# Sparse attention with a SoLU feed-forward layer: the first strided values loaded as two column halves for 128 partitions, not as two partition halves

## The chip, the cores and the metric

The kernel runs on one core of one Trainium2 chip. The metric is the device time of one execution in microseconds (us); lower is better. A core has five engines that run side by side and wait for each other by semaphores: TensorE (PE, matrix products), VectorE (DVE), ScalarE (ACT), GpSimd (POOL) and SyncE (SP). SyncE and ScalarE each issue transfers to a queue of their own; the packets of both queues are carried by the core's 16 DMA engines. SBUF is the memory on the chip, with 128 partitions; PSUM takes the products.

## The reference

Eight batches of eight heads with 576 positions and 64 elements a head. Heads 0 to 3 see the 32 latest positions ("local"), heads 4 to 7 see every 32nd earlier position ("strided"). The result goes through a feed-forward layer whose activation is x times softmax(x), with a layer norm behind it.

```python
scores = np.matmul(q, k.transpose(0, 1, 3, 2)) / np.sqrt(D)
mask_local = (rel >= 0) & (rel < 32)
mask_strided = (rel >= 0) & (pos[None, :] % 32 == pos[:, None] % 32)
scores = np.where(masks, scores, -1e9)          # heads 0-3 local, 4-7 strided
attn = softmax(scores)
x = np.matmul(attn, v)                          # -> 4608 tokens x 512
h = x @ w_in                                    # 512 -> 1024
solu = h * softmax(h)
ln = (solu - mean(solu)) / np.sqrt(var(solu) + 1e-6) * g_ln
out = ln @ w_out                                # 1024 -> 512
```

## The kernel before

The work goes by batch. A batch has five *units* of attention, two strided and then three local. A unit makes scores on TensorE (`qk`, a mask product at L512 and the scores at L517), takes the softmax on VectorE, ScalarE and GpSimd (L523 to L542), turns the probabilities by a transposing transfer (L546) and multiplies them by the values (`pv`, L568). Tiles of 128 tokens then go through the feed-forward layer (`ff`, L626 to L628 and L670 to L672, the bulk of TensorE's work).

The values are used as a high and a low fp16 part, with one scale for each batch, a power of two that is made from the squares of all values. For batch 0 the squares are summed on TensorE: `gram` (L379) multiplies each 128 columns of the raw values by themselves, 24 matmuls for the strided values and 10 for the local ones, in that order on TensorE ahead of and between the first scores.

The tile `vtwo` holds 12 x 4 x 64 float32 columns in 128 partitions. For batch 0 it holds the strided values twice: partitions 0 to 63 and 64 to 127 have the same content, and the columns are two halves y = 0, 1 of 1536. In HBM `vstr[0]` has 128 rows of 1536, row y x 64 + p. The split at L463 and L464 makes the high part for all 128 partitions, and the low part for the first 64, once for each y, without a transfer from one partition half to the other. For later batches the tile is used in another way: its first half takes the raw values (one load for 128 partitions), its second half the fp16 parts.

The order of work is written out by a planner (`Plan`): each step has an engine, a cost and a key, and the planner simulates queues to choose the order on each engine. `load` (L319) issues a transfer, on ScalarE's queue for the names in `ACTQ = {"t0", "t1"}`, which are the two loads of this case, otherwise on SyncE's queue. Steps carry names for what they read and write: `("vr", 1)` and `("vr2", 1)` are the first and the second of the two loads, and `gram` and the split are placed behind both. The semaphores themselves are set from the bytes that an instruction touches. There are eight semaphores for transfers (DMAHW0 to 7), dealt out in turn in the order of issue; the ninth transfer waits until the one that last had its semaphore is done.

At the start ScalarE issues the two loads, and SyncE issues strided `q`, the masks, strided `k`, the first `w_in` block, the local values (`vrl`), the second `w_in` block; then, with waits, `g`, local `k`, the third `w_in` block, local `q`, the fourth `w_in` block. The `w_in` blocks land in `room` and `eu` and are decoded on ScalarE and VectorE (L695 to L697).

Of the kernel before, what the change touches and what calls it, by code (L numbers as in the profile page):

```python
# [17 lines left out]
B, H, S, D = 8, 8, 576, 64  # L18
# [106 lines left out]
class Plan:  # L125
# [13 lines left out]
    def add(self, eng, dur, fn, key, r=(), w=(), lock=None, dma=None, after=()):  # L139

        n = len(self.steps)
        deps = set(after)
        for x in r:
            if x in self.writer:
                deps.add(self.writer[x])
        for x in w:
            if x in self.writer:
                deps.add(self.writer[x])
            deps.update(self.readers.get(x, ()))
        for x in r:  # L150
            self.readers.setdefault(x, []).append(n)
        for x in w:
            self.writer[x], self.readers[x] = n, []
        deps.discard(n)
        lock = eng == "pool" if lock is None else lock
        self.spaces.append({x[0] for x in (*r, *w) if isinstance(x, tuple) and x[0] in BANKED} if eng in ("pe", "act", "dve") else set())
        self.steps.append((eng, dur, fn, key, deps, lock, dma))
        return n
# [86 lines left out]
def attn_solu_kernel(ctx: ExitStack, tc: tile.TileContext, qloc, qstr, kloc, kstr, vloc, vstr, w_in, w_out, g, masks, out):  # L245
# [71 lines left out]
    def load(name, dst, src, us, key, w, after=()):  # L317
        e, q = ("act", nc.scalar) if name in ACTQ else ("sp", nc.sync)
        add(e, us, lambda: q.dma_start(dst, src), key, w=w, dma=LOAD, after=after)  # L319
# [104 lines left out]

    def load_v(b, a, key, key2=None):
        if b == 0 and a:
            for i in range(2):
                load(f"t{i}", vtwo[i * D : i * D + D].rearrange("p (y f) -> p y f", y=2), vstr[b].rearrange("(y p) f -> p y f", y=2), 1.95,
                     key2 if i else key, [("vr2", 1)] if i else [("vr", 1), ("v", 1, 0), ("v", 1, 1)])
            return  # L430
        load(f"v{a}{b}", vr_sb[a], (vloc, vstr)[a][b], (1.57, 1.93)[a], key, [("vr", a)])

# [323 lines left out]
    load_qk(0, 1, LF[0], LF[1])  # L756
    load_masks(LF[2])
    load_v(0, 1, LF[3], LF[4])
    load_v(0, 0, LF[5])
    load_qk(0, 0, LF[6], LF[7])  # L760
    load("g", g_sb, g, 0.1, LF[8], ["g"])
    prep_w()
    t = 0
    v_scale(0, VK[0])
    for b in range(B):
        if b:
            load_qk(b, 1, LK[b])
        v_split(b, 1, VK[b] + 0.5)
        for j in range(2):
            unit(b * NU + j, UK[b * NU + j], PK[b * NU + j])  # L770
        if b:
            load_qk(b, 0, LK[b] + 2)
        v_split(b, 0, VK[b] + 2.5)
        for j in range(2, NU - 1):
            unit(b * NU + j, UK[b * NU + j], PK[b * NU + j])
        if b + 1 < B:
            if b == 0:
                prep_o()
            load_v(b + 1, 1, LK[b + 1] + 0.5)
            load_v(b + 1, 0, LK[b + 1] + 2.5)  # L780
            v_scale(b + 1, VK[b + 1])
        unit(b * NU + NU - 1, UK[b * NU + NU - 1], PK[b * NU + NU - 1])
        if b == 0:
            split_o()
        while t < NT and (t * P + P - 1) // S <= b:
            ff(t, TK[t], GK[t])
            t += 1
# [63 lines left out]
```

## Time and profile before

| | |
|---|---|
| median of three runs | 514.79 us (513.05 to 514.99) |
| profiled execution | 512.79 us, span 511.1 us, mean granted clock 0.97 |
| TensorE busy | 473.5 us (93%) |
| VectorE busy | 358.5 us (70%) |
| ScalarE busy | 295.5 us (58%) |
| GpSimd busy | 157.4 us (31%) |
| moved by the DMA engines | 96.51 MB, mean 189 GB/s |

The span is one execution as the profiler records it; the profiled execution's own time contains it and what lies around it. The median of the runs stands 2.0 us above the profiled execution. A row of a group of instructions gives the line, the engine, the operation, what it writes and reads; behind it the busy time, and in brackets the idle time of its engine just before with what ended it. "SPq" and "ACTq" are the issuing sides of SyncE's and ScalarE's queues.

### The profile page before, as it was taken

The numbers are of one execution on the slowest core, as the hardware profiler recorded it, in microseconds if no ns is written. First come the engines' busy times: TensorE is split into PE (matmuls) and PEld (weight loads), VectorE is DVE, ScalarE is ACT, GpSimd is POOL, SyncE is SP. The second block draws the span as 40 slices with busy tenths as digits, with TensorE's granted clock in tenths as the row PEclk, the third lists the DMA queues.
The fourth block names the chain that finished last, engine by engine and source line by source line (L and its number), as shares of the span: only waits on it lengthen the run. The fifth ranks groups of instructions, "written<-read, shape, count | busy, mean of one in ns | idle before, by whom it ended". The sixth has DMA issues, their size and how long they took to land.

```text
span 511.1 us, 11878 instructions
## 1 busy us (share of the span) xinstructions
PE 473.5 (93%) x4858; PEld 247.2 (48%) x4858; DVE 358.5 (70%) x679; ACT 295.5 (58%) x414; POOL 157.4 (31%) x258
## 2 busy tenths in 40 slices
PE   0538978999999999999999999999999999999997
PEld 0435544445545555454544455555544555544443
DVE  0597989768767779667994789677975789754330
ACT  1578967684546737654765666564666447554331
POOL 3164363314313214313341235212531315311210
PEclk9855989999999999999999999999999999999999
DMA  8999999739993799979885499979985697673342
GB/s 218 402 310 271 355 211 202 152 77 242 273 199 84 157 211 280 222 212 195 236 161 109 118 227 239 245 202 223 231 158 104 164 167 158 108 122 63 65 104 78
DMA packets 168294, 96.51 MB, mean 189 GB/s; under 512 B 138032, under 2 KB 154800, under 8 KB 167728
## 3 DMA queue, kind: packets, MB, share of 16 engines
q1 hardware_dynamic: 162768, 84.74, 77.9%
q10 hardware_dynamic: 5472, 11.01, 6.9%
q8 instruction: 38, 0.62, 0.5%
q14 instruction: 16, 0.13, 0.1%
HBM read 40.03 MB, written 9.44 MB: 97 GB/s over the span
## 4 chain that ended last, share of the span: by engine, by line
PE 80%; DMA 7%; DVE 5%; ACT 4%; issue 2%; POOL 1%; ACTq 0%; POOLq 0%; DVEq 0%
PE h_ps L626 11%; PE o_ps L670 11%; PE h_ps L628 11%; PE h_ps L627 11%; PE o_ps L671 10%; PE o_ps L672 10%; PE s_ps L517 5%; PE x_ps L568 5%; DMA pt<-p 3%; DMA vtwo<-vstr 3%; PE s_ps L512 2%; DMA ct<-c 2%; POOL t L534 1%; ACT w L712 1%; PE s_ps L672 1%
## 5 line engine op out<-in xcount | busy, mean ns | idle before, releaser
L626 PE MATMUL h_ps<-w,xhi 128*128 128x512 f16 x280 | 107.1, 382 | 0.6 <-DVE eu L647 0.6
L627 PE MATMUL h_ps<-w,xhi 128*128 128x512 f16 x280 | 106.7, 381 | 0.0
L628 PE MATMUL h_ps<-w,xlo 128*128 128x512 f16 x280 | 106.6, 381 | 0.0
L670 PE MATMUL o_ps<-obuf,ct 128*128 128x512 f16 x272 | 103.4, 380 | 1.0 <-DMA ct<-c 1.0
L672 PE MATMUL o_ps<-obuf,ct 128*128 128x512 f16 x272 | 103.1, 379 | 0.0
L671 PE MATMUL o_ps<-obuf,ct 128*128 128x512 f16 x272 | 103.1, 379 | 0.0
L534 POOL TENSOR_TENSOR t<-t,m 128x576 f32<-128x576 f32 (+2 forms) x40 | 56.2, 1404 | 139.4 <-DVE m L531 111.4
L633 DVE TENSOR_REDUCE st<-h_ps 128x1 f32<-128x1024 f32 x35 | 42.8, 1222 | 42.5 <-PE h_ps L628 42.5
L652 DVE SCALAR_TENSOR_TENSOR c<-eu,st,c 128x1024 f16<-128x1024 f32 x36 | 48.8, 1354 | 25.3 <-ACT c L651 24.1
L644 ACT ACTIVATE eu<-h_ps,st,vsc 128x1024 f32<-128x1024 f32 x31 | 37.3, 1204 | 43.3 <-DVE st L634 43.3
L651 ACT ACTIVATE c<-eu,st 128x1024 f16<-128x1024 f32 x36 | 41.2, 1146 | 28.0 <-DVE st L650 26.0
L647 DVE SCALAR_TENSOR_TENSOR eu<-h_ps,st,eu 128x1024 f32<-128x1024 f32 x35 | 44.8, 1280 | 8.8 <-ACT eu L644 8.4
L660 POOL TENSOR_SCALAR st<-st 128x1 f32<-128x1 f32 x36 | 18.7, 520 | 103.2 <-ACT junk L654 102.0
L540 ACT CAST p<-t 128x576 f16<-128x576 f32 (+2 forms) x40 | 26.9, 674 | 33.2 <-POOL t L534 32.6
L628 PEld LDWEIGHTS <-xlo 128*128 128x128 f16 x288 | 28.3, 98 | 34.5 <-issue 0.8
L672 PEld LDWEIGHTS <-ct 128*128 128x128 f16 x288 | 28.2, 98 | 34.0
L626 PEld LDWEIGHTS <-xhi 128*128 128x128 f16 x288 | 28.2, 98 | 33.7 <-DVE eu L647 0.7
L670 PEld LDWEIGHTS <-ct 128*128 128x128 f16 x288 | 28.1, 98 | 33.1 <-DMA ct<-c 1.1
L627 PEld LDWEIGHTS <-xhi 128*128 128x128 f16 x288 | 28.3, 98 | 31.3 <-issue 0.6
L517 PE MATMUL s_ps<-k,q 64*54 64x54 f32 (+1 forms) x1280 | 41.4, 271 | 2.2 <-DMA q<-qloc 2.2
L671 PEld LDWEIGHTS <-ct 128*128 128x128 f16 x288 | 28.2, 98 | 30.2
L654 ACT ACTIVATE junk<-eu,st 128x1024 bf16<-128x1024 f32 x36 | 40.9, 1137 | 0.8 <-ACT ob L678 0.8
(148 smaller groups left out, 707.6 us busy)
## 6 DMA issues: line engine op xcount, KB each, us to landing
out<-ob ACTq DMA_DIRECT2D x36, 256.0 KB, 3.9
vtwo<-vstr SPq DMA_DIRECT2D x7, 768.0 KB, 6.6
vd<-vtwo SPq DMA_DIRECT2D x14, 384.0 KB, 8.8
vrl<-vloc SPq DMA_DIRECT2D x8, 640.0 KB, 5.6
q<-qstr SPq DMA_DIRECT2D x8, 594.0 KB, 5.4
k<-kstr SPq DMA_DIRECT2D x8, 594.0 KB, 6.8
k<-kloc SPq DMA_DIRECT2D x8, 576.0 KB, 6.0
q<-qloc SPq DMA_DIRECT2D x8, 576.0 KB, 4.2
```

Of the source, the lines that this page charges most:

```text
L517: nc.tensor.matmul(s_ps[row : row + nq, pair, i * nk : (i + 1) * nk], q_raw[half][hs, q0 : q0 + (nq - 1) * nqb + 1 : nqb], k_raw[half][hs, ...
L534: add("pool", nx * nk / 510 + 0.02, lambda: nc.gpsimd.tensor_tensor(tv, tv, sm.unsqueeze(2).broadcast_to([P, nx, nk]), op=ALU.mult), key + ...
L626: nc.tensor.matmul(hv[:, i], xhi[:, cc, tok], whi[:, cc, cols], start=(cc == 0), stop=False)
L627: nc.tensor.matmul(hv[:, i], xhi[:, cc, tok], wlo[:, cc, cols], start=False, stop=False)
L628: nc.tensor.matmul(hv[:, i], xlo[:, cc, tok], whi[:, cc, cols], start=False, stop=(cc == 3))
L633: add("dve", 1.21, lambda: nc.vector.tensor_reduce(low, hv, axis=AX.XY, op=ALU.max, negate=True), key + 0.2, r=HH, w=[(ST, "low")])
L647: add("dve", 1.3, lambda: nc.vector.scalar_tensor_tensor(uv, hv, ia, ev, op0=ALU.mult, op1=ALU.mult, accum_out=us), key + 0.3, r=[*HH, E, ...
L651: add("act", 1.2, lambda: nc.scalar.activation(c[:, 0], u, AF.Identity, bias=mean, scale=1.0), key + 0.35, r=[U, (ST, "mean")], w=[(C, 0)])
L652: add("dve", 1.28, lambda: nc.vector.scalar_tensor_tensor(c[:, 1], u, mean, c[:, 0], op0=ALU.add, op1=ALU.subtract), key + 0.4, r=[U, (ST, ...
L670: nc.tensor.matmul(o, ct[:, cc, :], ohi[:, cc, :], start=(cc == 0), stop=False)
L671: nc.tensor.matmul(o, ct[:, cc, :], olo[:, cc, :], start=False, stop=False)
L672: nc.tensor.matmul(o, ct[:, 8 + cc, :], ohi[:, cc, :], start=False, stop=(cc == 7))
```

## The change

The two loads of the first strided values are cut in another way. Before, load i went to partitions i x 64 to i x 64 + 63, with all 128 rows of the source as two runs of 1536 columns in each partition. After, load y goes to all 128 partitions, to columns y x 1536 to y x 1536 + 1535, and its source is the 64 rows of that y, read twice: the source's pattern has an outermost dim of 2 with step zero, then 64 rows, then 1536 columns. Both stay on ScalarE's queue with the same keys and names.

```diff
     def load_v(b, a, key, key2=None):
         if b == 0 and a:
-            for i in range(2):
-                load(f"t{i}", vtwo[i * D : i * D + D].rearrange("p (y f) -> p y f", y=2), vstr[b].rearrange("(y p) f -> p y f", y=2), 1.95,
-                     key2 if i else key, [("vr2", 1)] if i else [("vr", 1), ("v", 1, 0), ("v", 1, 1)])
+            for y in range(2):
+                f = slice(y * 6 * 4 * D, (y + 1) * 6 * 4 * D)
+                src = vstr[b][y * D : y * D + D].unsqueeze(0).broadcast_to([2, D, 6 * 4 * D])
+                load(f"t{y}", vtwo[:, f], src, 1.95, key2 if y else key, [("vr2", 1)] if y else [("vr", 1), ("v", 1, 0), ("v", 1, 1)])
             return
```

No step changes its place on an engine; what changes is which semaphores are waited for. ScalarE's first rows, with the shape that each transfer writes, are before:

```order
L846 UNCONDITIONAL_BRANCH
L319 DMA vtwo_72<-vstr 64x2x1536 x2
L695 ACT_TABLE_LOAD
L695 ACTIVATE ct_108<-room_68 128x1024
L696 ACTIVATE room_68<-room_68,consts_116 128x1024
L525 ACTIVATE t_87<-t_87 128x648
```

and after (the lines of the file have moved by one):

```order
L847 UNCONDITIONAL_BRANCH
L319 DMA vtwo_72<-vstr 128x1x1536 x2
L696 ACT_TABLE_LOAD
L696 ACTIVATE ct_108<-room_68 128x1024
L697 ACTIVATE room_68<-room_68,consts_116 128x1024
L526 ACTIVATE t_87<-t_87 128x648
```

The two stand first on ScalarE in both; only their shape differs. On TensorE the first of the 24 matmuls' weight loads in the Gram product waits, as the difference shows, for one transfer in place of two; the 13th, shown in the second piece, now has a wait of its own, for the second transfer:

```order
-L379 LDWEIGHTS vtwo_72 [waits DMAHW5_49,DMAHW0_49]
+L847 UNCONDITIONAL_BRANCH [waits barrier_Pool_Activation_PE_DVE_SP_release]
+L379 LDWEIGHTS vtwo_72 [waits DMAHW0_49]
 L379 MATMUL o_ps<-vtwo_72 128x128
 L379 LDWEIGHTS vtwo_72
```

```order
 L379 LDWEIGHTS vtwo_72
 L379 MATMUL o_ps<-vtwo_72 128x128
-L379 LDWEIGHTS vtwo_72
+L379 LDWEIGHTS vtwo_72 [waits DMAHW4_49]
 L379 MATMUL o_ps<-vtwo_72 128x128
 L379 LDWEIGHTS vtwo_72
```

So half of the product can start on the first transfer. On SyncE the rows are the same before and after, and read so in both:

```order
L319 DMA room_67<-w_in 128x2048
L319 DMA g_124<-g 128x8 [waits DMAHW0_49]
L319 DMA k_65<-kloc 128x1152 [waits DMAHW1_49]
L319 DMA eu_103<-w_in 128x2048 [waits DMAHW2_49]
L319 DMA q_63<-qloc 128x1152 [waits DMAHW3_49]
L319 DMA eu_104<-w_in 128x2048 [waits DMAHW4_49]
```

DMAHW0 belongs to the first of the two loads in both. DMAHW4, for which the fourth `w_in` block waits in the last row, belonged to the first `w_in` block before and belongs to the second of the two loads after.

## The prediction

> **What bounds the kernel now.** I read the page's shares first, then the span in three stretches, then the chain that ended last, and last the transfers of the opening.
>
> ```profile
> span 511.1 us, 11878 instructions
> PE 473.5 (93%) x4858; PEld 247.2 (48%) x4858; DVE 358.5 (70%) x679; ACT 295.5 (58%) x414; POOL 157.4 (31%) x258
> 0.00:14.55 14.55, 0.00 (x1) 0.03 (x1) 1.18 (x6) 1.28 (x1) 4.44 (x26) 1.00 0.90 230
> 14.55:65.00 50.45, 36.76 (x559) 25.60 (x563) 41.83 (x80) 42.02 (x49) 19.63 (x13) 0.73 1.06 333
> 65.00:511.10 446.10, 436.70 (x4303) 221.58 (x4299) 315.49 (x594) 252.19 (x364) 133.33 (x219) 1.00 0.83 171
> ```
>
> The last three rows are stretches: length, then the busy time of TensorE (PE), its weight loads, VectorE (DVE), ScalarE (ACT) and GpSimd (POOL), then granted clock, DMA share and GB/s. From 65 us on TensorE is busy 436.70 of 446.10 us, so it sets the pace and a delay that is handed to it at 65 us is never made up: at most 9.4 us is idle there, in pieces. Before 14.55 us TensorE does nothing at all. The chain says what it waits for:
>
> ```profile
> 0.79 0.74 ACTq L319
> ...
> 1.56 12.86 DMA vtwo<-vstr
> 14.41 0.14 issue
> 14.55 2.72 PE o_ps L379 x24
> 17.27 0.42 PE s_ps L512 x4
> 17.68 1.26 PE s_ps L517 x43
> 18.94 0.02 issue
> 18.96 0.85 DVE m L523
> ```
>
> Columns: start, length, what. The very two transfers that the change rewrites are the first link (12.86 us); behind them stand the 24 matmuls of the Gram product (L379), then the first scores (L512, L517), then VectorE's first reduction (L523). Everything else queues behind these in order:
>
> ```profile
> 17.17 1.19 ACT L695 ACTIVATE ct<-room 128x1024 f32<-128x1024 f32 x1 [13.68 <-DMA room<-w_in]
> 18.26 1.22 ACT L696 ACTIVATE room<-room,consts 128x1024 int32<-128x1024 uint32 x1
> 18.96 0.83 DVE L523 TENSOR_REDUCE m<-s_ps 128x12 f32<-128x648 f32 x1 [7.17 <-PE s_ps L517]
> 20.70 0.75 ACT L525 ACTIVATE t<-t 128x648 f32<-128x648 f32 x1 [1.22 <-DVE t L524]
> 20.00:30.00 10.00, 3.35 (x74) 2.50 (x74) 9.89 (x18) 8.83 (x9) 3.07 (x3) 0.63 1.02 414
> ```
>
> Only one decode of weights (1.19 + 1.22 us on ScalarE) can run ahead of the scores. VectorE's stream starts at L523 and is then busy 9.89 of 10 us: the opening is a serial stretch, and when the two transfers land, it starts.
>
> **The change part by part.** These are the transfers in flight while the two move, with KB and median us from issue to landing, and the count of packets on ScalarE's queue over the whole run:
>
> ```profile
> q10 hardware_dynamic: 5472, 11.01, 6.9%
> ...
> out<-ob ACTq DMA_DIRECT2D x36, 256.0 KB, 3.9
> room<-w_in SPq DMA_DIRECT2D x2, 1024.0 KB, 16.2
> eu<-w_in SPq DMA_DIRECT2D x2, 1024.0 KB, 13.7
> vtwo<-vstr ACTq DMA_DIRECT2D x2, 768.0 KB, 10.6
> vrl<-vloc SPq DMA_DIRECT2D x1, 640.0 KB, 15.6
> q<-qstr SPq DMA_DIRECT2D x1, 594.0 KB, 4.4
> k<-kstr SPq DMA_DIRECT2D x1, 594.0 KB, 13.0
> k<-kloc SPq DMA_DIRECT2D x1, 576.0 KB, 13.1
> q<-qloc SPq DMA_DIRECT2D x1, 576.0 KB, 13.0
> mask<-masks SPq DMA_DIRECT2D x1, 144.0 KB, 9.5
> 6.00:12.00 6.00, 0.00 (x0) 0.00 (x0) 0.98 (x4) 0.00 (x0) 0.00 (x0) 1.00 1.04 235
> 14.40:20.00 5.60, 5.15 (x86) 4.77 (x87) 1.00 (x2) 2.31 (x2) 0.00 (x0) 1.00 1.01 415
> ```
>
> *Bytes and rows.* Nothing changes: two transfers of 768 KB, 128 rows of 6,144 bytes each.
>
> *How a transfer is dealt out.* The queue's packets can be counted. Its 36 stores have 128 rows each, its two loads 64 partitions x 2 rows: 36 x 128 + 2 x 128 = 4,864 rows. 5,472 - 4,864 = 608 = 38 x 16. So each of the 38 transfers left exactly 16 packets more than its rows, one for each DMA engine: all were dealt over all 16. In each of them the outermost dim is 64 or 128, on both sides. After the change the destination's outermost dim is 128, but the source's is the pair of copies: `unsqueeze(0).broadcast_to([2, D, ...])` puts a dim of 2 with step zero ahead of the 64 rows. If a transfer is cut along the outermost dim of both its sides, there are only two parts, so two engines carry 64 rows each of either transfer, and fourteen carry none. No transfer of this trace has so short an outermost dim, so the trace doesn't decide this; a cut into 16 would need a second dim to be divided, and no count here calls for that. I take two engines as the likeliest.
>
> The Trainium skill, "DMA: Bandwidth & Descriptors", section "Why a DMA increments its semaphore by 16 and not by 1", states that the number of engines is the largest one up to 16 that divides the slowest dim of both patterns; its section "Rules for kernel authors" names a leading zero-stride broadcast as the case that confines a transfer to as many engines as there are copies. By that rule it is two engines here, the time of the sum below; the count of 16 closing packets agrees with the rule for 64 and 128, and no run so far shows it for 2.
>
> *What two engines cost.* The rate of one engine is 415 / 16 = 25.9 GB/s where all run freely (14.4 to 20 us) and 235 / 16 = 14.7 GB/s in the stretch in which the two transfers to 64 partitions run (6 to 12 us), though the engines are as busy (1.04). I take 25.9, since the new destination is that of the free stretch, all 128 partitions. The two busiest engines then carry:
> - both transfers: 2 x 768 KB / 2 = 786 kB, 30.4 us;
> - a sixteenth of what SyncE's queue has issued by 4.2 us (594 + 144 + 594 + 1024 + 640 + 1024 = 4020 KB), 257 kB, 9.9 us;
> - a sixteenth of what that queue issues once the first of the two has landed (576 + 1024 + 576 KB), 139 kB, 5.4 us.
>
> Sum 45.7 us. With the start at 1.56 us and about 1 us to close (a store of 256 KB needs 0.6 us at 415 GB/s and lands after 3.9, so issue and closing are 3.3 us at most), the second transfer lands at about 48.5 us in place of 14.41, the first (393 + 257 kB, 25.1 us) at about 28. Both queues' shares matter only in sum, so the order in which packets alternate cancels.
>
> Ends: if SyncE's packets took no time on the two engines, 30.4 us remain and it lands at 33; at 14.7 GB/s the sum is 80 us, and it lands at 83. The first is excluded by the rows (SyncE's loads ran beside the two all along), the second lies at the rate of a destination that is gone.
>
> *Waits on semaphores.* SyncE's issues wait on transfers of eight issues ago:
>
> ```profile
> SPq L319 <- DMA vtwo<-vstr: 5.0, 1, 5.0
> 9.23 0.33 SPq L319 DMA_DIRECT2D g<-g  x1
> ...
> 17.16 0.33 SPq L319 DMA_DIRECT2D eu<-w_in  x1
> ...
> 30.43 1.10 ACT L695 ACTIVATE c<-eu 128x1024 f32<-128x1024 f32 x1
> ```
>
> The issue of `g` waits for the first transfer (5.0 us now) and goes from 9.23 to about 28 us, with `kloc`, the third `w_in` and `qloc` behind it. The fourth `w_in`, which waited for the first `w_in`, now waits for the second transfer: 17.16 becomes about 48.5. Its 1024 KB then need 2.5 us at 415 GB/s plus 3.3, so it is there at 55; now ScalarE decodes it at 30.43, 13 us behind the end of the Gram product, which would be about 63. Covered.
>
> *The Gram product.* The first 12 of its 24 matmuls now need the first transfer alone and run at 28 us; the other 12 start with the second. Half of 2.72 us is off the path: 1.36 us gained.
>
> *What moves.* The product ends at 48.5 + 0.1 + 1.4 = 50.0 in place of 17.27: +32.7 us. Decoding the first weights ahead (2.4 us of ScalarE) buys nothing while VectorE has no gap; `q` for the first local unit no longer comes late:
>
> ```profile
> 27.77 1.25 PE L517 MATMUL s_ps<-k,q 64*64 64x96 f32 x24 [2.17 <-DMA q<-qloc]
> 29.40 0.74 DVE L523 TENSOR_REDUCE m<-s_ps 128x6 f32<-128x576 f32 x1
> ```
>
> That wait of 2.17 us ended before VectorE came to the scores (29.40), so it is hardly a gain either. Against this, after so long an idle stretch the clock may be at a half when the scores come (0.63 in 20 to 30 us); the scores at L517 then take 1.25 us for 24 where two units have 88, up to 2 us more. I leave both out, and keep 2 us to either side for the range. From 65 us on the whole pattern is the same, later by the same amount.
>
> The profiled execution has 512.79 us with a span of 511.1; 512.8 + 32.5 = 545.3. The median of the runs is 2.0 us above it, so **547 us**.
>
> **The rivals.** *Spread over 16 engines after all (faster).* If the cut goes by the destination's 128 rows, the slow stretch goes: for the two transfers' 1.57 MB and about as many SyncE packets in turn, 98 + 50 to 60 kB on each engine at 25.9 GB/s are 6 us, so both land at about 8.5 us, 6 us earlier. The mask (9.5 us to landing) and the first `w_in` come forward by 4 to 5, as they share the rate. That would give some 4.5 us: 510. It turns on one thing, 16 or 2 parts, and the count of packets will tell. The Trainium skill, "SBUF — State Buffer", section "Door 1: The DMA port swizzle", says that 64 partitions of one half reach only eight of 16 ports; the 235 against 415 GB/s agree with it, and it is the reason for which this rival would be faster.
>
> *Spread, but hidden.* The transfers land earlier, but the mask and the first weights don't, and VectorE starts its stream at 18 as before: 513.5 to 514.8, no change.
>
> *An uneven case.* The two transfers go to two different pairs of engines, or to four or eight: then 393 kB less on the worst engine, 15 us less, landing at 33: 531.
>
> **How the numbers follow.** Two engines 0.83: 547, its own range 535 to 560, by 12 us less where SyncE's share overlaps better and the engine is quicker alone, and 13 more where closing, clock or the rate (21 GB/s) is worse. Spread 0.10: 510. Spread but hidden 0.03: 514. Uneven 0.04: 531. Two runs of this kernel differ by up to 0.4%, so about 0.5% (2.6 us) is what can be told from no change. Faster 0.10, same 0.03, slower 0.87. To hold 8 in 10, two engines and the uneven case, the range is 530 to 561.
>
> **What the profile after would show.** ScalarE's queue with 5,472 - 2 x 14 = 5,444 packets if two engines close each of the two transfers, 5,472 if 16 do. The two with a median of about 36 us to landing. A DMA share that falls to about 2/16 between 33 and 47 us, with some 50 GB/s. The Gram product in two groups of 12, at about 28 and 48.5 us, and the scores behind the second. `g` issued at about 28, the fourth `w_in` at about 48. From 97 us on the same pattern as from 65. The prediction is wrong if the share stays at 1 until 12 us and TensorE starts before 14; its size is wrong if the second group starts far from 48, or if the stretch from there to full TensorE is not the 48 us that it is now.

## The result and the profile after

| | before | after |
|---|---|---|
| median of four runs | 514.89 us (513.05 to 515.87) | 551.79 us (550.61 to 553.62) |
| ratio | | 1.0724 (1.0682 to 1.0767) |
| span of the profiled execution | 511.1 us | 548.9 us |

The changed kernel is 36.9 us slower. On its page, the span, the busy time of each engine and the packets of ScalarE's queue:

```profile
span 548.9 us, 11878 instructions
...
PE 473.8 (86%) x4858; PEld 248.1 (45%) x4858; DVE 358.3 (65%) x679; ACT 295.1 (54%) x414; POOL 156.8 (29%) x258
...
q10 hardware_dynamic: 5444, 11.01, 5.8%
```

No engine has more work to speak of (TensorE 473.8 us, 473.5 before): the 37.8 us of the span are idle time. ScalarE's queue moved the same 11.01 MB with 28 packets less, two closing packets for each of the two transfers in place of 16. The chain of waits of after says where the time lies:

```profile
0.79 30.11 DMA vtwo<-vstr
30.90 0.05 issue
30.95 1.46 PE o_ps L379 x12
32.41 22.16 another core or an unknown queue
54.57 0.05 issue
54.62 1.46 PE o_ps L379 x12
56.08 0.41 PE s_ps L513 x4
56.49 1.21 PE s_ps L518 x37
```

The Gram product stands in two groups of 12, each behind a transfer. The piece that the chain can't name (32.41 to 54.57) is the second transfer: in the rows at the end of this section, TensorE (54.62) and SyncE (54.59) both end a wait for it at that time. The stretches of after, in the columns of before (the last three are clock, DMA share and GB/s):

```profile
0.00:54.62 54.62, 1.46 (x13) 1.20 (x13) 1.18 (x6) 3.48 (x3) 4.64 (x27) 1.00 0.47 145
54.62:103.00 48.38, 35.12 (x542) 24.79 (x543) 41.25 (x76) 39.15 (x47) 19.27 (x12) 1.00 0.83 250
103.00:548.90 445.90, 437.20 (x4306) 222.08 (x4304) 315.85 (x598) 252.48 (x365) 132.93 (x219) 1.00 0.82 172
6.00:14.00 8.00, 0.00 (x0) 0.00 (x0) 0.98 (x4) 0.00 (x0) 0.00 (x0) 1.00 1.02 303
18.00:30.00 12.00, 0.00 (x0) 0.00 (x0) 0.00 (x0) 2.20 (x2) 0.00 (x0) 1.00 0.13 53
32.00:40.00 8.00, 0.41 (x4) 0.14 (x2) 0.00 (x0) 0.00 (x0) 0.00 (x0) 1.00 0.97 249
42.00:54.00 12.00, 0.00 (x0) 0.00 (x0) 0.00 (x0) 0.00 (x0) 0.00 (x0) 1.00 0.12 52
```

From 18 to 30 us and from 42 to 54 us the share is 0.13 and 0.12, which is two engines of 16, and 53 GB/s are 26.5 for each of them. The steps behind that stretch are those of before, later: TensorE is busy 35.12 us of the 48.38 that follow (36.76 of 50.45 before), and 437.20 of 445.90 from then on. SyncE's waits, and the rows of the opening that depend on the two transfers:

```profile
SPq L319 <- DMA vtwo<-vstr: 49.0, 2, 27.1
30.92 0.33 SPq L319 DMA_DIRECT2D g<-g  x1
54.59 0.33 SPq L319 DMA_DIRECT2D eu<-w_in  x1
54.62 1.46 PE L379 MATMUL o_ps<-vtwo 128*128 128x128 bf16 x12 [22.21 <-DMA vtwo<-vstr]
57.77 0.83 DVE L524 TENSOR_REDUCE m<-s_ps 128x12 f32<-128x648 f32 x1 [47.37 <-PE s_ps L518]
69.24 1.10 ACT L696 ACTIVATE c<-eu 128x1024 f32<-128x1024 f32 x1
```

`g` waits for the first transfer and the fourth `w_in` block for the second. VectorE starts 38.8 us later than before (57.77 against 18.96); the span grew by 37.8, so 1.0 us was won back on the way, at a place that no run isolates.

### The profile page after: what moved, and what is told of

Its sections match the earlier page's. It is cut to its first block, busy times and chain, and to the rows that moved or that the text cites. A ratio compares the mean times of both kernels' runs of the same rounds, so it can differ in the third digit from the quotient of the medians.

```text
span 548.9 us, 11878 instructions
## 1 busy us (share of the span) xinstructions
PE 473.8 (86%) x4858; PEld 248.1 (45%) x4858; DVE 358.3 (65%) x679; ACT 295.1 (54%) x414; POOL 156.8 (29%) x258
## 3 DMA queue, kind: packets, MB, share of 16 engines
q10 hardware_dynamic: 5444, 11.01, 5.8%
## 4 chain that ended last, share of the span: by engine, by line
PE 75%; DMA 8%; ACT 5%; DVE 4%; another core or an unknown queue 4%; issue 2%; POOL 2%; ACTq 0%; POOLq 0%; DVEq 0%
PE h_ps L627 11%; PE o_ps L671 10%; PE h_ps L628 10%; PE h_ps L629 10%; PE o_ps L673 10%; PE o_ps L672 10%; DMA vtwo<-vstr 5%; PE s_ps L518 5%; PE x_ps L569 4%; PE s_ps L513 1%; DMA pt<-p 1%; POOL t L535 1%; DMA ct<-c 1%; ACT w L713 1%
## 5 line engine op out<-in xcount | busy, mean ns | idle before, releaser
L524 DVE TENSOR_REDUCE m<-s_ps 128x6 f32<-128x576 f32 (+2 forms) x40 | 30.3, 758 | 54.2 <-PE s_ps L518 53.9
L526 ACT ACTIVATE t<-t 128x576 f32<-128x576 f32 (+2 forms) x40 | 27.4, 686 | 59.9 <-DVE t L525 59.5
L652 ACT ACTIVATE c<-eu,st 128x1024 f16<-128x1024 f32 x36 | 41.2, 1146 | 28.4 <-DVE st L651 26.4
L379 PE MATMUL o_ps<-vtwo 128*128 128x128 bf16 x24 | 2.9, 306 | 53.2 <-DMA vtwo<-vstr 53.2
L673 PEld LDWEIGHTS <-ct 128*128 128x128 f16 x288 | 28.2, 98 | 34.0
L671 PEld LDWEIGHTS <-ct 128*128 128x128 f16 x288 | 28.1, 98 | 32.4 <-DMA ct<-c 0.5
```

Of the source, the lines that this page charges most:

```text
L652: add("act", 1.2, lambda: nc.scalar.activation(c[:, 0], u, AF.Identity, bias=mean, scale=1.0), key + 0.35, r=[U, (ST, "mean")], w=[(C, 0)])
L671: nc.tensor.matmul(o, ct[:, cc, :], ohi[:, cc, :], start=(cc == 0), stop=False)
L673: nc.tensor.matmul(o, ct[:, 8 + cc, :], ohi[:, cc, :], start=False, stop=(cc == 7))
```

## The experiments

The theory: a transfer is dealt out over as many engines as the outermost dims of both its sides allow, here two. The rivals: the rows are slow because each is read twice; or column halves to 128 partitions are slow as such. Kernels with the rows laid out twice in HBM (`vdup`) take another input of 1.5 MB for the first batch; the host only copies rows for it.

**Rows laid out twice, one dim of 128** (`double128`): `vdup[y]` has 128 rows, the 64 rows of y twice.

```diff
-                src = vstr[b][y * D : y * D + D].unsqueeze(0).broadcast_to([2, D, 6 * 4 * D])
+                src = vdup[y]
```

> The rows are laid out twice in HBM, so each of the two transfers reads 128 rows in one dim of 128 and writes the same 128 partitions and columns as the changed kernel. If the time went because a transfer is dealt out over as many engines as its outermost dim allows (2 in the changed kernel): 16 engines, 5472 packets on ScalarE's queue, a GB/s near 415 in the first 10 us, the Gram product at about 9 us, some 5 us less than the kernel before: 510. If the time went because two column halves to 128 partitions are slow as such: 551, as the changed kernel. If it went because rows are read twice from the same place: 510 as well.

Measured: 510.6 us, ratio to the kernel before 0.9934 (0.9911 to 0.9958). From its page, its stretches, TensorE's timeline and the chain:

```profile
q10 hardware_dynamic: 5472, 11.01, 6.3%
6.00:12.00 6.00, 3.99 (x64) 3.48 (x68) 0.98 (x4) 0.00 (x0) 0.00 (x0) 1.00 1.04 427
7.16 1.46 PE L379 MATMUL o_ps<-vtwo 128*128 128x128 bf16 x12 [7.16 <-DMA vtwo<-vdup]
9.47 1.46 PE L379 MATMUL o_ps<-vtwo 128*128 128x128 bf16 x12 [0.85 <-DMA vtwo<-vdup]
1.71 8.99 DMA k<-kstr
10.71 13.20 DMA q<-qloc
```

Same destination, same columns, same bytes as the changed kernel, and the loss is gone: the second transfer has landed by 9.47 us. It is the fastest kernel here. The Gram product's second group ends 6.3 us earlier than before (9.47 + 1.46 = 10.93, against 17.27), and 4.2 us of it arrive in the time: the chain now leads over strided `k`, which lands at 10.70, and local `q`, whose issue waits for it and which lands at 23.91.

**Rows laid out twice, still 2 x 64** (`gap2`): a real step in place of the zero one. Here `vdup` is 2 x 2 x 65 x 1536, and row 64 of each copy is unused.

```diff
+                src = vdup[y][:, 0:D]
```

> The rows are laid out twice in HBM with one unused row between the copies, so the source is 2 x 64 rows, its outermost dim 2 with a real step, and no row is read twice. Dealing by the outermost dim: 2 engines, 5444 packets, second transfer at 54.6 us, 551 to 552 as the changed kernel. If reading the same rows twice was the cost: about 510.

Measured: 551.82 us, ratio 1.073 (1.0695 to 1.0765), the time of the changed kernel. Its page, a stretch and TensorE's timeline:

```profile
q10 hardware_dynamic: 5444, 11.01, 5.7%
20.00:30.00 10.00, 0.00 (x0) 0.00 (x0) 0.00 (x0) 1.66 (x2) 0.00 (x0) 1.00 0.13 53
54.62 1.46 PE L379 MATMUL o_ps<-vtwo 128*128 128x128 bf16 x12 [21.94 <-DMA vtwo<-vdup]
```

Nothing is read twice here, and the second transfer lands at the same 54.6 us. So neither the repeated rows nor the zero step cost the time: the outermost dim of 2 does, which `double128` hasn't.

**A repeat of 16, and of 4** (`repeat16`, `repeat4`). The edit of `repeat16` is shown; `repeat4` has 4 in place of 16.

```diff
+                src = vstr[b][y * D : y * D + P // 16].unsqueeze(0).broadcast_to([16, P // 16, 6 * 4 * D])
```

> Reads 8 rows 16 times in place of 64 rows twice (so the first batch's strided values are others), with a zero step in an outermost dim of 16. Dealing by the outermost dim: 16 engines, 5472 packets, both transfers landed by 10 us, 510. If a zero step or repeated rows cost the time: 551 or more, since a row is read 16 times.

Measured: 514.14 us, ratio 1.001 (0.9985 to 1.0034): the loss is gone, as the theory says, but not the 510 that it gave.

```profile
q10 hardware_dynamic: 5472, 11.01, 6.6%
6.00:12.00 6.00, 1.46 (x12) 1.19 (x12) 0.98 (x4) 0.00 (x0) 0.00 (x0) 1.00 1.01 242
```

All 16 engines close the transfers and are busy (1.01), and move 242 GB/s, not 427.

> Reads 32 rows 4 times (so the first batch's strided values are others). Dealing by the outermost dim: 4 engines, 36*144 + 256 + 8 = 5448 packets; the four carry 393 kB of the two transfers, 15.2 us, and 9.9 us of SyncE's first loads, with some 3 to 6 us for slow stretches and the rest of SyncE's loads: second transfer at 28 to 34 us, 528 to 534. If repeated rows cost the time: more than 551.

Measured, one run: 536.84 us, above the expected 528 to 534. From its page, its stretches and the chain:

```profile
q10 hardware_dynamic: 5448, 11.01, 6.1%
6.00:12.00 6.00, 0.00 (x0) 0.00 (x0) 0.00 (x0) 0.00 (x0) 0.00 (x0) 1.00 1.02 238
1.97 38.69 DMA vtwo<-vstr
```

The count is the 5448 of four engines, and the time lies between those of 2 and of 16, as it should. The landing at 40.7 us is later than the 34 that I allowed: the engines moved 238 GB/s, not 415, in the stretch in which SyncE's first loads ran beside, and the second transfer took 16 us more behind the first, which let `g` go out at 24.65 us. How the excess divides between the two stretches wasn't taken apart, and it is one run.

**16 groups of 8 rows, nothing repeated** (`gap16`), to tell the two causes of the slow 242 GB/s apart. Here `vdup` is 2 x 16 x 9 x 1536, and row 8 of each group is unused.

```diff
+                src = vdup[y][:, 0 : P // 16]
```

> The same values as the reference's, laid out twice in HBM as 16 groups of 8 rows with an unused row between groups: the source's outermost dim is 16 with a real step, and no row is read twice. 16 engines and 5472 packets by every theory. The kernel that read 8 rows 16 times also had 16 engines, but moved only 242 GB/s from 6 to 12 us and gained nothing (514.1). If its slow rate came from reading the same rows again and again: here some 425 GB/s and 510. If it comes from which engine writes which partitions (a source of two dims is dealt out in another way than one of 128 rows): about 240 GB/s and 514.

Measured: 513.38 us, ratio 0.9986 (0.9958 to 1.0014).

```profile
6.00:12.00 6.00, 1.46 (x12) 1.20 (x12) 0.98 (x4) 0.00 (x0) 0.00 (x0) 1.00 1.02 241
```

As slow as the repeat. So it isn't the reading of the same rows; what differs from `double128` is that the 128 rows stand in two dims, 16 x 8, with an unused row behind each group.

**The rest of the loads behind the second transfer** (`late_rest`), for the size of the loss. A small transfer that reads the second half of `vtwo` is put ahead of `g`.

```diff
+    (peek,) = buf("peek", [P, 8])
+    add("sp", 0.1, lambda: nc.sync.dma_start(peek, vtwo[:, 6 * 4 * D : 6 * 4 * D + 8]), LF[8] - 0.001, r=[], w=["peek"], dma=LOAD)
     load("g", g_sb, g, 0.1, LF[8], ["g"])
```

> The changed kernel, with one more small transfer on SyncE's queue that reads 8 columns of the second half of vtwo, ahead of g: so g, local k, the third w_in block and local q wait until the second transfer has landed and share no engine with it. If SyncE's packets on the two engines are what the term of 5.4 us left too small: the first transfer at 30.9 as before, the second after 64 more rows at 0.235 us each, 15.0 us, and closing, at 46.5 in place of 54.6; the loads behind it come later but are covered until about 56 to 60; 544 in all. If the second transfer is slow by itself: 54 and 551 to 554.

Measured: 543.81 us, ratio to the kernel before 1.0563 (1.0506 to 1.062), 8 us less than the changed kernel. TensorE's timeline, and a stretch behind the second transfer:

```profile
31.30 1.46 PE L379 MATMUL o_ps<-vtwo 128*128 128x128 bf16 x12 [31.30 <-DMA vtwo<-vstr]
46.24 1.46 PE L379 MATMUL o_ps<-vtwo 128*128 128x128 bf16 x12 [13.48 <-DMA vtwo<-vstr]
50.00:54.00 4.00, 1.95 (x50) 1.60 (x48) 3.93 (x10) 2.87 (x3) 0.00 (x0) 1.00 1.01 423
```

Alone on its two engines the second transfer takes 14.9 us (46.24 - 31.30), as 64 rows at 26 GB/s do; beside SyncE's loads it took 23.7 (54.62 - 30.95). And those loads, with the fourth `w_in` block behind them, move 423 GB/s once the second transfer is out of the way; beside it both together moved 249 (32 to 40 us of the changed kernel).

**Four transfers of 64 rows** (`quarters`, `quarters2`), for the rate to 64 partitions. The names that each of the four transfers writes are left out here ("...").

```diff
+                for i in range(2):
+                    load(f"t{y}", vtwo[i * D : i * D + D, f], vstr[b][y * D : y * D + D], 0.98, ...)
```

> Four transfers of 64 rows to 64 partitions each, both sides in one dim of 64; 16 engines, 36*144 + 256 + 64 = 5504 packets. If the rate of 235 GB/s belongs to 64 partitions at a time: last of the four at about 14 us, 513 to 515, less up to 1.4 us for the first half of the Gram product. If it belongs to a source or destination of two dims: 425 GB/s and about 510. The local values and the second w_in block are issued later here, since two more semaphores are taken; they are wanted after 18 us only.

Measured: 561.85 us, ratio 1.0926 (1.086 to 1.0992). This is inconclusive on the time: four steps in place of two made the planner write out another order of work, with the Gram product behind the first scores. Only the rate can be read; it is 241 GB/s from 6 to 12 us. The second version issues two transfers in one step of the planner:

```diff
+                def both(y=y, f=f):
+                    for i in range(2):
+                        nc.scalar.dma_start(vtwo[i * D : i * D + D, f], vstr[b][y * D : y * D + D])
```

> Each of the two loads is issued as two transfers of 64 rows to 64 partitions, both sides in one dim of 64, as one step of the planner, so that the order of all other work stays that of the changed kernel (where four separate steps had moved it: 561.9). 16 engines, 5504 packets. If the rate goes by which engine writes which partition, 64 rows to 64 partitions are as slow as 2 x 64: about 240 GB/s from 6 to 12 us, the second pair landed by 14 to 16 us, 513 to 516. If a single dim on both sides is enough: some 425 GB/s and 510. Two more semaphores are taken, so the local values and the second w_in block are issued 2 to 4 us later.

Measured: 515.69 us, ratio 1.0025 (1.0005 to 1.0045). Its stretches and TensorE's timeline:

```profile
6.00:12.00 6.00, 1.12 (x11) 1.16 (x12) 0.97 (x4) 0.00 (x0) 0.00 (x0) 1.00 1.03 232
12.00:16.00 4.00, 0.31 (x3) 0.04 (x1) 0.00 (x0) 0.00 (x0) 0.00 (x0) 1.00 1.04 247
17.48 1.44 PE L379 MATMUL o_ps<-vtwo 128*128 128x128 bf16 x12 [5.17 <-DMA vtwo<-vstr]
```

One dim on both sides, but of 64: slow again, 232 to 247 GB/s. The second pair landed 1.5 us later than I allowed.

## Why the prediction was right, and where it was off

**Two engines: shown.** The count of 5,444 packets, the share of about 2/16 at some 50 GB/s and the two groups of the Gram product came as forecast, at later times (the share from 42 to 54 us, where 33 to 47 had been given). That the outermost dim of 2 causes it is shown from both sides: `gap2` keeps the dim without repeating a row and has the whole loss, `double128` keeps destination, columns and bytes without that dim and has none. The rule of the Trainium skill, "DMA: Bandwidth & Descriptors", section "Why a DMA increments its semaphore by 16 and not by 1", agrees with the counts for 2 (5,444), 4 (5,448) and 16 (5,472).

**The landing: the term that was too small.** 48.5 us were forecast and 54.6 measured. The transfers' own term holds: 15.2 us for 64 rows, 14.9 alone in `late_rest`. What was mis-sized is the rate beside SyncE's loads, which I took as 25.9 GB/s for each engine because the destination has 128 partitions. While both queues ran, all engines were busy but moved 303 GB/s (6 to 14 us) and 249 (32 to 40): 18.9 and 15.6 for each engine. So the first transfer came 2.9 us later than the 28 forecast, and SyncE's second lot cost 23.7 - 14.9 = 8.8 us where the term had 5.4. That is 6.3 us in all, the difference between 54.6 and 48.5 but for rounding; `late_rest` takes the second lot out and wins 8 us. The prediction had set the slow rate of before, 14.7 GB/s for each engine, aside as "the rate of a destination that is gone"; 15.6 came with the new destination. So that slow rate was no sign of 64 partitions alone. The range held because it had left room for a rate of 21 GB/s.

**The Gram product.** Half of it was off the path: 1.46 of its 2.92 us ran at 31 us. Forecast 1.36 for the 12; right.

**The waits on semaphores: covered, as forecast.** The fourth `w_in` went out at 54.59 and was decoded at 69.24, which is 14.6 us after the wait ended; ScalarE came from its own work there.

**The clock.** I kept 2 us to either side; the 48 scores behind the Gram product took as long as before (1.42 us by the timelines of both), so nothing is seen of it at that place. The clock column is no help here: it reads 1.00 all through the opening of after and 0.73 in this stretch before, yet in the trace of after the 24 local scores take 1.17 us at 64.19 and 0.83 us at 103.59, both under a reading of 1.00.

**To the end.** The delay at VectorE's first step, 38.8 us, is the 32.7 of the forecast and the 6.1 by which the second transfer landed later than forecast. (The last step of the sum carries 32.5 on, 0.2 less, without a reason.) It arrives at the end but for 1.0 us; medians differ by 36.9. In its last 446 us TensorE idles 8.7 us, where it idled 9.4 before, so next to nothing was made up there.

**The rivals.** The price of the spread was right (510 against 510.6 in `double128`, landing at 9.5 where 8.5 was worked out), its condition wasn't: I let it turn on 16 or 2 engines alone. `repeat16` and `gap16` have 16 engines and 128 partitions and gain nothing, 514.1 and 513.4. The reason given there, the ports that 64 partitions reach, can't be the whole one. The uneven case was priced too low for four engines: landing at 33 and 531 us, where `repeat4` landed at 40.7 and took 536.8.

## What to carry to other kernels

Look at the outermost dim of both sides of a transfer, as it is issued: a short one, such as two copies ahead of the rows, left all but two of 16 DMA engines without a part here, and the count of closing packets in the profile (packets less rows) shows how many took part. Of the shapes tried only one had the full rate: 128 rows in one dim on both sides, which laying the rows out twice in HBM gave, for 0.9934 of the time before. And a transfer that was late at the start of this serial opening was paid almost in full (37.8 of 38.8 us), since TensorE was busy nearly all the time behind it.

## What the runs showed of the hardware that was not expected

With all 16 engines busy, the opening moved 427 GB/s where the two transfers had 128 rows in one dim, but 241 with 16 x 8 rows, 235 with 64 x 2 and 232 with 64. The two transfers have the same bytes in all of them, in rows of 6,144 bytes. The Trainium skill, "DMA: Bandwidth & Descriptors", section "The descriptor swizzle", says that in a transfer to 128 partitions each engine writes partitions of a port of its own. The 427 fit that, and another assignment for the other shapes could explain the slow ones; but the trace names no engine for a packet, so this cause is a guess, not shown.

A transfer on two engines slowed the other fourteen as well: 303 and 249 GB/s at a share of 1.02 and 0.97. Even if the fourteen had moved all of the 249, that is 17.8 for each, where in `late_rest` the same loads alone ran at 423, 26.4 for each of 16. What slows them no run shows.
